# Sums through x's page by ScalarE, S1 and S2 ahead of two transposes, weights in one piece, one subtraction on VectorE

## The chip, the cores and the metric

One Trainium2 chip, one of its cores. The metric is the time of one execution of the whole program in device microseconds (us); 791.16 us is the median of three runs of the kernel before (791.1 to 791.66). A core has five engines that each work through a queue of their own: TensorE (PE; its weight loads are shown apart as PEld), VectorE (DVE), ScalarE (ACT), GpSimd (POOL) and SyncE (SP, which here only starts DMAs). They wait for one another by semaphores. SBUF is the on-chip memory, PSUM the memory of TensorE's results, in eight banks of 512 float32 columns on 128 partitions.

## The reference

Attention with a mask by blocks of 64, and then a feed-forward part with a gate across positions. 8 batches, 8 heads, 576 positions, 64 columns per head, 512 columns of the model, 1024 of the feed-forward part.

```python
def _attn_ref(q, k, v):
    scores = scale * np.matmul(q, k.transpose(0, 1, 3, 2))
    mask = block_i >= block_j                      # pos // 64
    scores = np.where(mask, scores, -1000000000.0)
    attn = np.exp(scores - np.max(scores, axis=-1, keepdims=True))
    attn = attn / (np.sum(attn, axis=-1, keepdims=True) + 1e-09)
    return np.matmul(attn, v)

def _moe_ref(x, w_in, g_ln, w_sg, b_sg, w_out):
    h = gelu(x @ w_in)                             # the tanh form
    u, v = h[..., :512], h[..., 512:]
    v_n = (v - mean(v)) / np.sqrt(var(v) + 1e-06) * g_ln
    v_s = np.einsum('ts,bsd->btd', w_sg, v_n) + b_sg[None, :, None]
    return x + (u * v_s) @ w_out
```

## The kernel before

**Slots.** The program has 32 slots, one for each pair of heads of a batch. Slot n turns the exponents of pair n into its attention output and computes the scores of pair n+1; four slots make a batch. After each batch its feed-forward part is laid out in pieces (`hole`), which the next slots spread between their attention steps. So the first four slots hold attention alone, and from the fifth on every slot has products of the feed-forward part between its steps.

**Accuracy.** Scores and feed-forward products are made of three passes of a fast format: high part by high part, high by low and low by high. For q and k the high part `qk_h` is a CAST on DVE of both together (1152 columns), and the low part `qk_l` is the difference, two subtractions of 576 columns on POOL (`split_qk`, lines 127 to 135). It is made in slot n for pair n+2, so the scores of the next slot need it. A pair's q and k come in by two DMAs on SP, issued at the start of slot n for pair n+2.

**A slot's steps on PE.** `turn0`: the first column block of the exponents of both heads is transposed into two banks named pa (a bank for each head, four transposes each). `turn2`: the third and fourth column blocks into pb. S1 and S2 (`step1`, `step2`): scores of the next pair, into banks s. Block 0 (`av0`): value product with the first column block, into ob. `turn1`: the second and last column blocks into pc. `turn_first`: the two 64x64 corners into pd. S3 and S4: the rest of the next pair's scores. `av2`: value products of pb. `turn_sums`: the inverse row sums, spread over columns by POOL in `rx`, are transposed into pd (128 columns) and pe (512). `av1`: value products of pc. `av00`: the corner's product, also into pd. Each transposed bank is copied to SBUF as pt: pa, pb of the first head by ACT and of the second by DVE, both pc by ACT. Scores get their row maximum on DVE (CUSTOM_DVE, six for S1 and S2, six for S3 and S4), then their exponential on ACT (prob).

**Banks.** Five PSUM banks carry the tag s (scores, ob, accumulators of the feed-forward part), three the tag p (pa, pb, pc, pd, pe, in turn). A new tile of a tag waits until the third tile of p before it, or the fifth of s, has been read for the last time.

**End of a slot.** `normalise` (line 492): ACT copies ob and pd's corner product into a page x, and DVE multiplies x by the inverse sums in pe and pd. `split` makes a high part xh of x on DVE (CAST) and low parts on POOL, for the feed-forward part. SP writes x out to spill.

**Weights.** The feed-forward weights come in during the first nine slots (`WS`, line 731, steps per slot: 2, 2, 2, 1, 10, ...). A weight step fetches a piece by DMA four steps ahead, and unpacks it: `w_in` and `w_out` are double precision, so ACT scales the high words (w<-raw), DVE shifts and merges (TENSOR_SCALAR and two SCALAR_TENSOR_TENSOR on 256 columns), ACT casts the high part (wi_h<-w) and POOL subtracts the low part (wi_l). `load_share` hands a slot's steps out at four places in quarters.

**Order.** PE runs in program order, pinned (`kept`). DVE, ACT, POOL and SP are ordered by a scheduler that takes what it expects to be ready first, within data and buffer dependences; `issue_after` keeps a weight step behind the latest maximum and exponential.

Of the kernel before, what the change touches and what calls it, by code (L numbers as in the profile page):

```python
# [9 lines left out]
F32 = mybir.dt.float32  # L10
# [4 lines left out]
ALU = mybir.AluOpType  # L15
# [13 lines left out]
def kernel(  # L29
# [13 lines left out]
    B, H, D, S = qT.shape  # L43
    P = 128
    BLK = 64
# [23 lines left out]
    def page(dtype, n, name):  # L69
        tag, bufs = KINDS.get(name, KINDS["w"])  # L70
        return sp.tile([P, n], dtype, tag=tag, name=name, bufs=bufs)

    def bank(tag, name, bufs):
        return psum.tile([P, 512], F32, tag=tag, name=name, bufs=bufs)

    def sbank(name):
        return bank("s", name, 5)

    def pbank(name):
        return bank("p", name, 3)  # L80
# [3 lines left out]
    def pin(ins, e):  # L84
        return tc.keep_in_program_order(ins) if e in kept else ins
# [4 lines left out]
    def turn(out, in_, identity):  # L90
        return pin(nc.tensor.transpose(out, in_, identity), "P")  # L91
# [11 lines left out]
    V, A, G, SP = Pinned(nc.vector, "V"), Pinned(nc.scalar, "A"), Pinned(nc.gpsimd, "G"), Pinned(nc.sync, "S")  # L103

    def copy(e, dst, src):
        return {"v": V.tensor_copy, "a": A.copy, "g": G.tensor_copy}[e](dst, src)
# [8 lines left out]
    def load_qk(n):  # L115
        b, h = PAIRS[n]
        if n == 0:

            q_f, k_f = page(F32, S, "w"), page(F32, S, "w")
        else:  # L120
            t = sp.tile([P, 2, S], F32, tag="qk_f", name="qk_f", bufs=1)
            q_f, k_f = t[:, 0, :], t[:, 1, :]
        SP.dma_start(q_f, qT[b, h : h + 2].rearrange("a d s -> (a d) s"))
        SP.dma_start(k_f, kT[b, h : h + 2].rearrange("a d s -> (a d) s"))
        qk[n] = (q_f, k_f) if n == 0 else t

    def split_qk(n):
        t = qk[n]
        hi = sp.tile([P, 2, S], F32R, tag="qk_h", name="qk_h", bufs=1)
        lo = sp.tile([P, 2, S], F32R, tag="qk_l", name="qk_l", bufs=1)  # L130
        V.tensor_copy(hi, t)
        for i in (1, 0):
            G.tensor_tensor(lo[:, i, :], t[:, i, :], hi[:, i, :].bitcast(F32), op=ALU.subtract)
        q_h, k_h, q_l, k_l = hi[:, 0, :], hi[:, 1, :], lo[:, 0, :], lo[:, 1, :]
        qk[n] = [(q_h, k_h), (q_h, k_l), (q_l, k_h)]

    def load_v(n):
        b, h = PAIRS[n]
        v_f = v_bufs[n % 2]
        cols = slice(h * D, (h + 2) * D)  # L140
        SP.dma_start(
            v_f[:, : NT - 1, :],
            v[b, : (NT - 1) * P, cols].rearrange("(j p) d -> p j d", p=P),
        )
        SP.dma_start(v_f[:TAIL, NT - 1, :], v[b, S - TAIL :, cols])
        vals[n] = v_f
# [6 lines left out]
    t = sbank("warm")  # L153
# [15 lines left out]
    for s in (0, 1):  # L169
        t = cp.tile([P, NT, 2 * D], F32, name=f"v_f{s}")  # L170
# [5 lines left out]
    for s in range(4):  # L176
        row = []
        for i in range(NT):
            t = cp.tile([P, P * (i + 1) if i else BLK], F32, name=f"prob{s}_{i}")
# [106 lines left out]
    def weight_step():  # L286

        with ExitStack() as stack:
            for ins in newest.values():
                stack.enter_context(tc.issue_after(ins.ins))  # L290
            while weights and next(weights[0][1], None) is None:
                weights.popleft()
# [96 lines left out]
    class Values:  # L389
# [71 lines left out]
        def turn_sums(self):  # L461

            turn(self.t4[:, 128:256], self.rx[:, 0, :], ident)
            t = self.rp = pbank("pe")
            for i in range(1, NT):
                turn(t[:, (i - 1) * P : i * P], self.rx[:, i, :], ident)

        def av(self, dst, j, pts, c0, n, start, stop):
            for a in (0, 1):
                r = slice(a * D, (a + 1) * D)  # L470
                mm(dst[r, :], self.v[:, j, r], pts[a][:, c0 : c0 + n], start=start, stop=stop)
# [19 lines left out]

        def normalise(self):

            x = self.x = page(F32, S, "x")
            copy("a", x[:, BLK:], self.ob)
            copy("a", x[:, :BLK], self.o0)
            V.tensor_tensor(x[:, BLK:], self.rp, x[:, BLK:], op=ALU.mult)
            V.tensor_tensor(x[:, :BLK], self.t4[:, 128:192], x[:, :BLK], op=ALU.mult)
            spill[self.b, self.p] = dp.tile([P, S], F32, tag="spill", name="spill", bufs=12)
            SP.dma_start(spill[self.b, self.p], x)  # L500

# [14 lines left out]
    def run_side(k):  # L516

        while k > 0 and side and side[0][0] != "G":
            k -= 1
            side.popleft()[1]()  # L520

    def run_gelu():

        if side and side[0][0] == "G":
            side.popleft()[1]()
# [196 lines left out]
    def hole(k=1):  # L722

        while k > 0 and work:
            try:
                next(work[0])
                k -= 1
            except StopIteration:
                work.popleft()

    WS = [2, 2, 2, 1, 10, 3, 3, 3, 2]

    def load_share(n, k):

        if n < len(WS):
            for _ in range(WS[n] * (k + 1) // 4 - WS[n] * k // 4):
                weight_step()

    PLAN = ["1111111", "1111111", "1111111", "1111112"]
# [3 lines left out]
    def slot(n, sc):  # L743
        va = Values(n, sc)
        nx = Scores(n + 1) if n + 1 < N else None
        g = [int(x) for x in (FIRST if n // 4 == 1 else PLAN)[n % 4]]
        if n + 2 < N:
            load_qk(n + 2)
        if n + 1 < N:
            load_v(n + 1)  # L750
        va.inverse()
        va.turn0(0)
        va.turn0(1)
        hole(g[0])
        load_share(n, 0)
        run_side(2)

        va.turn2()
        va.turn2_rest()
        if nx:  # L760
            nx.step1()
            nx.step2()
        va.av0()
        if nx:
            nx.exponents(1, 4)
        va.turn1()
        hole(g[1])
        load_share(n, 1)
        run_side(2)
        hole(g[2])  # L770
        run_side(2)
        va.turn1_rest()
        va.turn_first()
        if nx:
            nx.step3()
            nx.step4()
        va.av2()
        va.turn_sums()
        if nx:
            nx.exponents(3, 0, 2)  # L780
        hole(g[3])
        load_share(n, 2)
        run_side(2)
        va.av1()
        va.av00()
        hole(g[4])
        va.normalise()

        wait = n // (H // 2) > 0 and n % (H // 2) < 2
        pending.append(va.split)  # L790
        if not wait:
            while pending:
                pending.popleft()()
        run_side(2)
        if n + 2 < N:
            split_qk(n + 2)
        load_share(n, 3)
        hole(g[5])
        run_gelu()
        run_side(3)  # L800
        hole(g[6])
        run_side(3)
        if n % (H // 2) == 1:
            while pending:
                pending.popleft()()
        return nx
# [13 lines left out]
    sc.step4()  # L820
    sc.exponents(2)
    split_qk(1)
    for _ in range(2):
        weight_step()
    kept.difference_update("VA")
    for n in range(N):
        sc = slot(n, sc)
        if n % (H // 2) == H // 2 - 1:

            def begin(b=PAIRS[n][0]):  # L830
                v_, u_, s_, o_ = feed_forward(b)

                work.extend([v_, u_, *last_o, s_])
                last_o[:] = [o_]

            begin()
# [45 lines left out]
```

## Time and profile before

| | |
|---|---|
| median of three runs | 791.16 us (791.1 to 791.66) |
| the profiled execution | 792.08 us, of which the span from first to last instruction 790.2 us |
| mean granted clock of PE | 0.978 of full speed |
| PE busy | 761.1 us, 96% |
| DVE busy | 499.7 us, 63% |
| ACT busy | 450.0 us, 57% |
| POOL busy | 267.9 us, 34% |

The durations in this document are from the one profiled execution. A row of the timeline is: start, duration, engine, line, operation, output<-inputs, shape, count, and in brackets the idle time before it and what ended it. All instructions that the kernel issues through its helpers carry the helper's line (L88 products, L91 transposes, L101 the other engines), so they are told apart by tile names. A row of the windows is: start and end, then the length, and busy time with the number of instructions for PE, PEld, DVE, ACT and POOL, the granted clock, the DMA share and GB/s. A row of the waits is: who waited, for whom, total us, how often, and the longest. A row of the groups is: line, engine, operation, tiles, shapes, count, busy us, mean ns, and the idle time before.

### The profile page before, as it was taken

The page shows a single profiled execution, that of the slowest core. Times are in us where ns is not written, and L with a number is a line of the kernel's source. Part 1 is how long each engine was busy: PE and PEld are TensorE (multiplying, and loading weights), DVE is VectorE, ACT ScalarE, POOL GpSimd, SP SyncE. Part 2 cuts the span into 40 slices and gives each one's busy share as a digit, 9 for nine tenths or more (in the row PEclk, how much of TensorE's full clock was granted, in tenths as well). Part 3 has the DMA queues.
Part 4 walks back from the last instruction along what each step waited for, and adds up shares of the span by engine and source line. Part 5 has one row for each costly group of instructions (what it writes and reads, how often), then busy time and mean ns, then how long its engine had stood idle before and what let it go on. Part 6 is the DMA issues. An engine that isn't in the chain of part 4 may idle for free. (4 is left out here: it accounts for less than half of the span.)

```text
span 790.2 us, 15821 instructions
## 1 busy us (share of the span) xinstructions
PE 761.1 (96%) x5926; PEld 639.9 (81%) x5926; DVE 499.7 (63%) x1457; ACT 450.0 (57%) x1172; POOL 267.9 (34%) x331
## 2 busy tenths in 40 slices
PE   7777998999999999999999999999999999999998
PEld 5554786877888888887888888888888978888998
DVE  5897578885757466563866648565676647633532
ACT  4775689567844478435974368544793358721600
POOL 4354255552424113351133414231233510322121
PEclk9897799999999999999999999999999999999999
DMA  7143224212241024311042122410233101320042
GB/s 239 61 126 118 89 91 141 88 61 75 78 149 60 2 76 122 106 61 52 25 136 90 61 76 62 145 50 32 77 106 121 61 19 59 105 76 31 1 121 75
DMA packets 46911, 65.66 MB, mean 83 GB/s; under 512 B 4082, under 2 KB 22514, under 8 KB 46836
## 3 DMA queue, kind: packets, MB, share of 16 engines
q1 hardware_dynamic: 46836, 64.67, 25.6%
q8 instruction: 46, 0.75, 0.4%
q14 instruction: 29, 0.24, 0.1%
HBM read 45.78 MB, written 18.87 MB: 82 GB/s over the span
## 5 line engine op out<-in xcount | busy, mean ns | idle before, releaser
L101 ACT ACTIVATE prob<-prob,negm 128x448 f32<-128x448 f32 (+4 forms) x320 | 176.4, 554 | 40.6 <-DVE negm L101 37.1
L101 POOL TENSOR_TENSOR qk_l<-qk_f,qk_h 128x576 fp32r<-128x576 f32 x62 | 90.9, 1486 | 229.7 <-PE pe L91 92.2
L101 DVE CUSTOM_DVE_ANT_0 prob<-s,mask 128x288 f32<-128x288 f32 (+2 forms) x320 | 117.1, 421 | 56.3 <-PE s L88 56.1
L88 PE MATMUL ob<-pt,v_f 128*64 128x512 f32 (+4 forms) x640 | 107.1, 448 | 0.0
L88 PE MATMUL s<-qk_h 64*128 64x288 f32 (+1 forms) x372 | 88.4, 341 | 3.9 <-ACT u L101 3.7
L101 POOL TENSOR_TENSOR gl<-u,gh 128x288 fp32r<-128x288 f32 x64 | 51.9, 812 | 113.4 <-DVE gh L101 80.2
L88 PE MATMUL s<-qk_l,qk_h 64*128 64x288 f32 (+1 forms) x372 | 83.0, 303 | 0.0
L88 PE MATMUL accu<-xh,wi_h 128*128 128x288 f32 x256 | 78.1, 305 | 0.0
L88 PE MATMUL accs<-ws_h,vh 128*128 128x288 f32 x256 | 78.1, 305 | 0.0
L88 PE MATMUL s<-qk_h,qk_l 64*128 64x288 f32 (+1 forms) x372 | 78.0, 300 | 0.0
L88 PE MATMUL acco<-gh,wo_h 128*128 128x288 f32 x256 | 77.6, 303 | 0.0
L88 PE MATMUL accu<-xl,wi_h 128*128 128x288 f32 x256 | 75.7, 296 | 0.0
L88 PE MATMUL accu<-xh,wi_l 128*128 128x288 f32 x256 | 75.5, 295 | 0.0
L88 PE MATMUL accs<-ws_l,vh 128*128 128x288 f32 x256 | 75.5, 295 | 0.0
L88 PE MATMUL accs<-ws_h,vl 128*128 128x288 f32 x256 | 75.5, 295 | 0.0
L88 PE MATMUL acco<-gh,wo_l 128*128 128x288 f32 x256 | 75.4, 294 | 0.0
L88 PE MATMUL acco<-gl,wo_h 128*128 128x288 f32 x256 | 75.3, 294 | 0.0
L88 PEld LDWEIGHTS ob<-pt,v_f 128*64 128x64 f32 x640 | 37.8, 137 | 41.2 <-issue 32.2
L88 PE MATMUL accv<-wi_h,xh 128*128 128x512 f32 x160 | 66.0, 412 | 3.3 <-POOL xh L101 3.3
L88 PEld LDWEIGHTS s<-qk_h 64*128 64x128 f32 x372 | 63.7, 188 | 5.9 <-ACT u L101 4.9
L88 PEld LDWEIGHTS s<-qk_h,qk_l 64*128 64x128 f32 x372 | 63.8, 187 | 0.0
L88 PE MATMUL accv<-wi_l,xh 128*128 128x512 f32 x160 | 63.8, 399 | 0.0
(104 smaller groups left out, 1924.2 us busy)
## 6 DMA issues: line engine op xcount, KB each, us to landing
spill<-x SPq DMA_DIRECT2D x32, 288.0 KB, 3.7
xr<-spill SPq DMA_DIRECT2D x32, 288.0 KB, 3.2
out_T<-xr SPq DMA_DIRECT2D x32, 288.0 KB, 3.0
qk_f<-in_qT SPq DMA_DIRECT2D x31, 288.0 KB, 3.4
qk_f<-in_kT SPq DMA_DIRECT2D x31, 288.0 KB, 3.8
v_f<-in_v SPq DMA_DIRECT2D x32, 256.0 KB, 3.1
raw<-in_w_in SPq DMA_DIRECT2D x16, 256.0 KB, 4.7
raw<-in_w_out SPq DMA_DIRECT2D x8, 256.0 KB, 5.2
```

The source lines that it names most:

```text
L88: return pin(nc.tensor.matmul(*a, **k), "P")
L101: return lambda *a, **k: pin(f(*a, **k), self.letter)
```

## The change

Four edits, in three groups. In `split_qk` the two subtractions on POOL become one on DVE over both halves. In `turn_sums` the transposed sums are copied by ACT from pe and pd into the page x at once, and `normalise` then multiplies x by ob and by the corner product on DVE, with nothing left for ACT; before, ACT copied ob and the corner, and DVE multiplied by pe and pd. In the first four slots `turn2` stands behind S1, S2 and block 0 rather than ahead of them, and a slot's weight steps are all handed out at the second place rather than in quarters.

```diff
@@ split_qk
-        for i in (1, 0):
-            G.tensor_tensor(lo[:, i, :], t[:, i, :], hi[:, i, :].bitcast(F32), op=ALU.subtract)
+        V.tensor_tensor(lo, t, hi.bitcast(F32), op=ALU.subtract)
@@ turn_sums
-            t = self.rp = pbank("pe")
+            t = pbank("pe")
             for i in range(1, NT):
                 turn(t[:, (i - 1) * P : i * P], self.rx[:, i, :], ident)
+
+            x = self.x = page(F32, S, "x")
+            copy("a", x[:, BLK:], t)
+            copy("a", x[:, :BLK], self.t4[:, 128:192])
@@ normalise
-            x = self.x = page(F32, S, "x")
-            copy("a", x[:, BLK:], self.ob)
-            copy("a", x[:, :BLK], self.o0)
-            V.tensor_tensor(x[:, BLK:], self.rp, x[:, BLK:], op=ALU.mult)
-            V.tensor_tensor(x[:, :BLK], self.t4[:, 128:192], x[:, :BLK], op=ALU.mult)
+            x = self.x
+            V.tensor_tensor(x[:, BLK:], self.ob, x[:, BLK:], op=ALU.mult)
+            V.tensor_tensor(x[:, :BLK], self.o0, x[:, :BLK], op=ALU.mult)
@@ load_share
-            for _ in range(WS[n] * (k + 1) // 4 - WS[n] * k // 4):
+            share = WS[n] * (k + 1) // 4 - WS[n] * k // 4
+            if n < H // 2:
+
+                share = WS[n] if k == 1 else 0
+            for _ in range(share):
                 weight_step()
@@ slot
-        va.turn2()
-        va.turn2_rest()
+        early = n < H // 2
+        if not early:
+            va.turn2()
+            va.turn2_rest()
         if nx:
             nx.step1()
             nx.step2()
         va.av0()
+        if early:
+            va.turn2()
+            va.turn2_rest()
```

In the three places shown next, numbers behind a name (prob_3_132, v_f_105) tell one buffer from another, and x2 means two such instructions in a row.

On PE, at the start of the second slot, before, from the last pa to pc:

```order
L91 MATMUL pa<-ident,prob_1_137 128x128
L91 MATMUL pb<-ident,prob_4_134 128x128
L91 MATMUL pb<-ident,prob_3_132 128x128
...
L91 MATMUL pb<-ident,prob_3_141 128x64
L88 MATMUL s<-qk_h 128x288 x2
...
L88 MATMUL s<-qk_h,qk_l 128x288 x2
L88 MATMUL ob<-pt,v_f_105 64x512 x2
L91 MATMUL pc<-ident,prob_4_134 128x128
```

The same place now:

```order
L91 MATMUL pa<-ident,prob_1_137 128x128
L88 MATMUL s<-qk_h 128x288 x2
...
L88 MATMUL s<-qk_h,qk_l 128x288 x2
L88 MATMUL ob<-pt,v_f_105 64x512 x2
L91 MATMUL pb<-ident,prob_4_134 128x128
L91 MATMUL pb<-ident,prob_3_132 128x128
...
L91 MATMUL pb<-ident,prob_3_141 128x64
L91 MATMUL pc<-ident,prob_4_134 128x128
```

The ten transposes into pb now stand between block 0's product and pc; nothing else on PE has moved.

On ACT, from the end of the first slot into the second, before (x<-ob and x<-pd are the copies of `normalise`):

```order
L101 ACTIVATE w<-raw 128x256
L101 COPY x<-ob 128x512
L101 COPY x<-pd 128x64
L101 COPY pt<-pa 128x512
L101 CAST wi_h<-w 128x256
L101 COPY pt<-pb 128x512
L101 ACTIVATE prob_1_110,sums<-prob_1_110,negm 128x192
L101 ACTIVATE prob_1_119,sums<-prob_1_119,negm 128x192
L101 ACTIVATE prob_4_116,sums<-prob_4_116,negm 128x576
L101 ACTIVATE prob_4_125,sums<-prob_4_125,negm 128x576
L101 ACTIVATE w<-raw 128x256
L101 COPY pt<-pc 128x512 x2
```

The same place now:

```order
L101 COPY x<-pe 128x512
L101 COPY pt<-pa 128x512
L101 ACTIVATE prob_1_110,sums<-prob_1_110,negm 128x192
L101 ACTIVATE prob_1_119,sums<-prob_1_119,negm 128x192
L101 ACTIVATE prob_4_116,sums<-prob_4_116,negm 128x576
L101 ACTIVATE prob_4_125,sums<-prob_4_125,negm 128x576
L101 ACTIVATE w<-raw 128x256 x2
L101 COPY pt<-pb 128x512
L101 COPY pt<-pc 128x512
L101 CAST wi_h<-w 128x256
L101 COPY pt<-pc 128x512
```

The copy of pb, which stood ahead of the four exponentials, now stands behind them and behind two weight steps' first operation; the weight operations around the slot's start are gone.

On DVE, at the same place in the second slot, before:

```order
L101 CAST qk_h<-qk_f 128x1152
L101 TENSOR_SCALAR w<-raw 128x256
L101 SCALAR_TENSOR_TENSOR w<-raw,w 128x256
L101 TENSOR_TENSOR ri<-sums,tiny 128x10
L101 RECIPROCAL ri<-ri 128x10
L101 SCALAR_TENSOR_TENSOR w<-w 128x256
L101 TENSOR_TENSOR x<-pe,x 128x512
L101 TENSOR_TENSOR x<-pd,x 128x64
L101 CAST xh<-x 128x576
L101 COPY pt<-pa 128x512
L101 COPY pt<-pb 128x512
```

The same place now, up to the first maximum of S1:

```order
L101 CAST qk_h<-qk_f 128x1152
L101 TENSOR_TENSOR qk_l<-qk_f,qk_h 128x1152
L101 TENSOR_TENSOR x<-pd,x 128x64
L101 TENSOR_TENSOR ri<-sums,tiny 128x10
L101 TENSOR_TENSOR x<-ob,x 128x512
L101 RECIPROCAL ri<-ri 128x10
L101 COPY pt<-pa 128x512
L101 CAST xh<-x 128x576
L101 ISA prob_4_116,negm<-s,mask 128x288
```

The low part's subtraction is new behind the CAST, the three weight operations and the copy of pb have left this stretch, and the multiplies read ob and pd's corner. The copy of pb stands here behind the six maxima and three weight operations, at this place:

```order
L101 ISA prob_4_125,negm<-s,mask,negm 128x288
L101 ISA negm 128x1
L101 TENSOR_SCALAR w<-raw 128x256 x2
L101 SCALAR_TENSOR_TENSOR w<-raw,w 128x256
L101 COPY pt<-pb 128x512
L101 SCALAR_TENSOR_TENSOR w<-raw,w 128x256
L101 SCALAR_TENSOR_TENSOR w<-w 128x256 x2
L101 ISA prob_3_114,negm<-s,mask 128x448
```

Two weight steps now follow one another there, where before one stood alone.

## Prediction

> **What bounds the kernel now.** I read the clock row of the page first, then a long window from the middle, then the list of what TensorE waited for.
>
> ```profile
> PEclk9897799999999999999999999999999999999999
> ...
> 300.00:400.00 100.00, 99.56 (x800) 84.94 (x799) 63.55 (x183) 60.19 (x154) 35.92 (x41) 1.00 0.26 82
> ...
> PE pa L91 <- ACT pt L101: 6.1, 4, 1.9
> PE pb L91 <- DVE x L101: 3.7, 3, 1.4
> ...
> PE accv L88 <- POOL xh L101: 3.3, 1, 3.3
> ```
>
> Each digit of the first row is 20 us: the granted clock is below full only in the first seven slices. In the window from 300 to 400 TensorE (PE, first pair of numbers) is busy 99.56 of 100 us at clock 1.00, with DVE at 64 and ACT at 60. So from about 140 us on, nothing but PE's own work sets the end, and the change adds or removes no product. What can move is the start: the four slots without feed-forward products, and the fifth. Time won before PE is full is won once and kept.
>
> The slots are measured from one first product of S3 to the next. A name is tile<-operands, then shape, count, and in brackets the idle time before it and what ended it.
>
> ```profile
> 14.44 1.71 PE L91 MATMUL pb<-ident,prob 128*128 128x128 f32 x7
> 15.87 0.42 PE L88 MATMUL s<-qk_h 64*128 64x288 f32 x1
> ...
> 17.46 1.08 PE L88 MATMUL ob<-pt,v_f 128*64 128x512 f32 x4
> 18.47 1.08 PE L91 MATMUL pc<-ident,prob 128*128 128x128 f32 x7
> ...
> 20.07 0.47 PE L88 MATMUL s<-qk_h 64*128 64x448 f32 x1 [0.19 <-DVE negm L101]
> ...
> 37.24 0.45 PE L88 MATMUL s<-qk_h 64*128 64x448 f32 x1
> ...
> 38.84 1.08 PE L88 MATMUL ob<-pt,v_f 128*64 128x320 f32 x8
> ...
> 41.68 0.66 PE L91 MATMUL pa<-ident,prob 128*128 128x128 f32 x4
> 43.64 0.66 PE L91 MATMUL pa<-ident,prob 128*128 128x128 f32 x4 [1.30 <-ACT pt L101]
> 45.61 1.08 PE L91 MATMUL pb<-ident,prob 128*128 128x128 f32 x7 [1.31 <-DVE x L101]
> ...
> 51.48 0.44 PE L88 MATMUL s<-qk_h 64*128 64x448 f32 x1
> ...
> 65.82 0.44 PE L88 MATMUL s<-qk_h 64*128 64x448 f32 x1
> ...
> 78.83 0.80 PE L88 MATMUL accv<-wi_h,xh 128*128 128x512 f32 x1 [3.26 <-POOL xh L101]
> ```
>
> S3 stands at 20.07, 37.24, 51.48 and 65.82: periods of 17.2, 14.2 and 14.3. At full clock the pieces are S1+S2 1.6 (15.87 to 17.46), block 0's products 1.0 (to 18.47), S3+S4 1.6, from there to the next pa 2.8 (38.84 to 41.68), and some 3 for the transposes: about 10. The rest is the pair of waits at each slot's start (1.30 and 1.31 here) and the half clock after them. In the third group the two waits have these causes:
>
> ```profile
> 38.37 0.62 DVE L101 CUSTOM_DVE_ANT_0 prob<-s,mask 128x448 f32<-128x448 f32 x1 [0.62 <-PE s L88]
> ...
> 40.57 0.75 DVE L101 CAST qk_h<-qk_f 128x1152 fp32r<-128x1152 f32 x1
> ...
> 41.56 1.58 DVE L101 SCALAR_TENSOR_TENSOR w<-raw,w 128x256 uint32<-128x256 uint32 x1
> 43.07 1.36 DVE L101 TENSOR_TENSOR ri<-sums,tiny 128x10 f32<-128x10 f32 x1
> ...
> 41.45 2.95 POOL L101 TENSOR_TENSOR qk_l<-qk_f,qk_h 128x576 fp32r<-128x576 f32 x2 [1.57 <-PE pe L91]
> ...
> 39.03 0.67 ACT L101 ACTIVATE prob<-prob,negm 128x448 f32<-128x448 f32 x1
> ...
> 42.44 0.56 ACT L101 COPY x<-ob 128x512 f32<-128x512 f32 x1
> 43.01 0.58 ACT L101 COPY pt<-pa 128x512 f32<-128x512 f32 x1
> ```
>
> While POOL subtracts (41.45 to 44.40), two DVE operations that read SBUF take 1.58 and 1.36, the second for ten columns. They stand in front of the multiply by pe, which frees pe's PSUM bank for pb. The second pa waits for ACT's copy of the first, since pd and pe hold the other two banks.
>
> **The change, part by part.** (1) *Low parts on DVE.* POOL's 2.95 goes, and with it the two held operations, about 2.2 per slot on DVE. DVE gets one subtraction of 1152 columns, which no row shows. Below it stands the CAST of that width (0.75), above it POOL's 2.95. I work it out from one DVE operation in two widths:
>
> ```profile
> L101 DVE CUSTOM_DVE_ANT_0 prob<-s,mask 128x448 f32<-128x448 f32 x64 | 39.5, 617 | 47.2 <-PE s L88 47.0
> ...
> L101 DVE COPY pt<-pb 128x512 f32<-128x512 f32 x32 | 21.9, 685 | 7.2 <-PE pb L91 6.6
> ...
> L101 DVE CUSTOM_DVE_ANT_0 prob<-s,mask 64x64 f32<-64x64 f32 x64 | 13.5, 211 | 0.0
> ```
>
> (617-211)/384 is 1.06 ns a column and 0.14 fixed, so 1.36, nearer the CAST than POOL. At 0.75 each of three slots would gain 0.6 more; at 2.95 each would lose 1.6.
>
> (2) *Sums through x's page.* The same two ACT copies, of pd and pe now, before the exponents end; pe's bank comes free on ACT, before DVE's multiply. New waits: the last product into pd follows ACT's copy of pd, and the next block-0 product needs DVE's multiply of ob. Walked from S3 at 0 (DVE's first maximum at 1.13 and CAST at 3.33, ACT's first exponent at 1.79, all from the rows above): ACT copies pd at about 4.5 and pe at 5.5, DVE ends the subtraction at 5.3, the pd multiply at 5.5, ob's at 6.2. PE would reach the last pd product at 4.3 and waits 0.3; the second pa waits 0.3 for pe's copy; S1 starts at 6.0 with q and k split. Two waits of 1.3 become two of 0.3. Behind the subtraction on DVE stand the copy of the second pa and the cast of x, so the maxima start at about 7.3.
>
> (3) *S1 and S2 before pb.* Maxima start earlier, but pb is now copied late: in ACT's order its copy stands behind four exponents and two weight multiplies, in DVE's behind six maxima, two shifts and one merge. pc's second half takes the bank that DVE's copy frees.
>
> ```profile
> 33.47 0.46 DVE L101 CUSTOM_DVE_ANT_0 prob<-s,mask 128x288 f32<-128x288 f32 x1 [0.52 <-PE s L88]
> ...
> 35.66 0.29 DVE L101 TENSOR_SCALAR w<-raw 128x256 uint32<-128x256 uint32 x1
> 35.99 0.43 DVE L101 SCALAR_TENSOR_TENSOR w<-raw,w 128x256 uint32<-128x256 uint32 x1
> ...
> 34.25 0.46 ACT L101 ACTIVATE prob<-prob,negm 128x192 f32<-128x192 f32 x1 [1.26 <-DVE negm L101]
> ...
> 36.88 0.41 ACT L101 ACTIVATE w<-raw 128x256 f32<-128x256 f32 x1
> ```
>
> Six maxima take 2.2 (33.47 to 35.66), two shifts and a merge about 1.0, the copy 0.69: from 7.3 that is 11.2. PE, after S1, S2, block 0 and pb, has only three transposes of pc left and stands from 9.95 to 11.25: a **new wait of 1.3** in mid-slot. ACT's copy (exponents from 0.78 behind the first maximum, 2.63 long, two multiplies 0.7, copy 0.58) is done at 12.0 and just frees pd. S3 comes at 12.35. That is the second slot's successor: 12.35 against 14.24.
>
> (4) *First slot.* Here pc's second half needs ACT's copy of pb. S1 starts at 14.44, where pb stood; PE is through S1, S2, block 0, pb and half of pc at 19.2. DVE copies the second pa at 14.7 and has two weight pieces to unpack, so maxima run from 17.25 to 19.8, exponents to 21.0, two multiplies to 21.7, a CAST that waits for DVE to 22.2, the copy to 22.8. **PE waits 3.7 us**; S3 moves from 20.07 to 23.75.
>
> (5) *Slots after it.* The slot behind that wait runs S3 at half clock until 26.1: 13.1 instead of 17.17. The next 12.35 instead of 14.24. In the fourth slot one weight step is left, with one DVE cast and no ACT work ahead of the copies: 11.75 instead of 14.34. S3 of the fourth slot: 23.75+13.1+12.35+11.75 = 60.95 against 65.82, won 4.9. There the feed-forward block waits for POOL's xh, before 13.0 behind S3; now three shifts, the subtraction, the merges and three weight splits on POOL lead to 12.45, won 0.5. Behind it stands half clock before (the row of 80.70 below); it becomes shorter, and I count 0.3. Hand-overs that the walk leaves out cost 0.1 in each of four slots. Sum: 4.9+0.5+0.3-0.4 = **5.3 us**. From the profiled execution (792.08 with a span of 790.2) that is 786.8; the median of the runs shown lies 0.92 lower, so **785.9**. The later 28 slots I count at 0, within 1 either way: a block of products stands between each new wait and the work that it holds. Input loads on SP still run one slot ahead of their use.
>
> **Rivals.** (a) *The clock.* The granted clock goes in steps of 3.4 us:
>
> ```profile
> 12.40:15.80 3.40, 2.69 (x12) 2.42 (x12) 2.10 (x4) 2.02 (x8) 2.95 (x4) 0.52 0.20 74
> ...
> 22.60:26.00 3.40, 2.30 (x21) 1.33 (x19) 3.37 (x15) 3.40 (x13) 0.83 (x2) 1.00 0.01 2
> 26.00:29.40 3.40, 1.09 (x6) 0.62 (x6) 3.36 (x5) 2.31 (x8) 3.06 (x4) 1.00 0.29 87
> 29.40:32.90 3.50, 2.83 (x20) 2.50 (x22) 2.81 (x6) 0.91 (x2) 2.98 (x4) 0.53 0.75 246
> ...
> 43.10:46.50 3.40, 1.55 (x12) 1.14 (x13) 3.33 (x8) 0.89 (x3) 2.81 (x4) 1.00 0.54 162
> ...
> 80.70:84.10 3.40, 3.40 (x27) 2.79 (x26) 2.28 (x7) 0.74 (x3) 0.00 (x0) 0.50 0.86 328
> ```
>
> A step with PE busy 1.09 or 1.55 is followed by half clock, one with 2.30 is not. The new wait leaves about 2.1 of 3.4, between them. If it costs the next step, S3 and S4 run at half clock and each of three periods grows by 0.85: 2.5 lost, less 1.0 since the fifth slot's half clock lies partly in its wait: 787.4. The Trainium skill's page "TensorE: Matmul & The Clock Gate", Part 4 (PE-mode transpose), says that transposes do not count as PE work for the clock; by that rule the stretch of pb, wait and pc counts as idle and this rival holds, at 787.4. This case speaks both ways: the step at 12.40 holds transposes alone and full clock follows (pb to 15.87, S1 then at 0.42), the step at 29.40, half transposes, is followed by more half clock.
>
> (b) *The lock moves.* POOL's split of x (576 columns, half of the 2.95) now runs beside DVE's maxima and ends about where the shifts start. If it ends later, shift and merge are held as 1.58 and 1.36 show: 1.3 in each of three slots, won 1.4: 789.8. The page "SBUF — State Buffer", section "SBUF: two separate sides", calls it an exclusive lock for whole instructions; the trace agrees.
>
> (c) *Slower: the wait for pb's copy is as long in each slot as in the first.* It decides from 1.3+1.8 = 3.1 us a slot on. At 3.7, and 0.85 for the half clock, three slots lose 9.75 more: 795.6. For it: ACT's in-order queue and weights in mid-slot. Against it: from the second slot on the bank hangs on DVE's copy, which stands ahead of most unpacking.
>
> (d) *More.* If the fifth slot loses one step of half clock less (3.4 us at half speed, 1.7) and the subtraction takes the CAST's 0.75 (three slots by 0.6, 1.8): 3.5 more, 782.4.
>
> **Chances.** Forecast 0.42, clock 0.20, more 0.13, lock 0.13, slower 0.12. A measurement here can tell about 0.2% (1.6 us). Forecast, clock and more count as faster, 0.75; lock as the same, 0.13; slower 0.12. The range 781.5 to 790.5 leaves out the slower case and the far ends, under 2 in 10.
>
> **What would show it.** pa's second wait and S1's start near 0.3 instead of 1.3; no pb wait for DVE; a wait of pc for DVE's or ACT's pt of 3 to 4 us in the first slot and 1 to 1.5 in the next three; S3 of the fourth slot near 61; DVE's qk_l at 1.36; the clock row of the third to fifth slice above 7. I am wrong if pc waits over 3 in later slots, if the subtraction takes near 3, or if PE below 99% appears after 140 us.

## The result and the profile after

The changed kernel takes 784.45 us (median of four runs, 783.3 to 785.17) against 791.41 us of the kernel before measured with it (791.1 to 791.82): a ratio of 0.991, interval 0.9896 to 0.9925. That is 7.0 us won where 5.3 were forecast. The profiled execution took 783.98 us, its span is 782.2. The page of the changed kernel opens with:

```profile
span 782.2 us, 15752 instructions
...
PE 756.5 (97%) x5926; PEld 636.9 (81%) x5926; DVE 497.0 (64%) x1488; ACT 448.1 (57%) x1172; POOL 182.5 (23%) x269
...
PEclk8898999999999999999999999999999999999999
```

POOL is 85 us less busy. DVE now does the subtraction in 42 us and yet is no busier than before (497.0, before 499.7). The clock row is still below full only in the first seven slices.

PE's waits in the first five slots of the changed kernel, by its timeline, with the first product of S3 of each slot between them:

```profile
23.14 1.20 PE L91 MATMUL pc<-ident,prob 128*128 128x128 f32 x4 [2.61 <-ACT pt L101]
...
24.17 0.72 PE L88 MATMUL s<-qk_h 64*128 64x448 f32 x1
...
36.88 0.94 PE L91 MATMUL pc<-ident,prob 128*128 128x128 f32 x7 [0.88 <-DVE pt L101]
...
37.88 0.47 PE L88 MATMUL s<-qk_h 64*128 64x448 f32 x1
...
49.18 0.94 PE L91 MATMUL pc<-ident,prob 128*128 128x128 f32 x7 [1.02 <-DVE pt L101]
...
50.09 0.47 PE L88 MATMUL s<-qk_h 64*128 64x448 f32 x1
...
55.21 0.34 PE L88 MATMUL pd<-pt,v_f 128*64 128x64 f32 x4 [0.77 <-ACT x L101]
...
61.11 0.75 PE L91 MATMUL pc<-ident,prob 128*128 128x128 f32 x4 [0.53 <-DVE pt L101]
...
61.73 0.45 PE L88 MATMUL s<-qk_h 64*128 64x448 f32 x1
...
74.46 0.80 PE L88 MATMUL accv<-wi_h,xh 128*128 128x512 f32 x1 [4.77 <-POOL xh L101]
```

The pair of waits of 1.3 at each slot's start is gone from the second slot on; what remains there is 0.8 or less. In its place stands the wait of pc in mid-slot, 2.61 in the first slot and 0.5 to 1.0 after it. From S3 to S3 a slot takes 13.7, 12.2 and 11.6 us instead of 17.8, 14.2 and 14.3.

### The profile page after: what moved, and what is told of

The parts are those of the page before. It is cut to its first block, busy times and chain, and to the rows that moved or that the text cites. A ratio compares the mean times of both kernels' runs of the same rounds, so it can differ in the third digit from the quotient of the medians.

```text
span 782.2 us, 15752 instructions
## 1 busy us (share of the span) xinstructions
PE 756.5 (97%) x5926; PEld 636.9 (81%) x5926; DVE 497.0 (64%) x1488; ACT 448.1 (57%) x1172; POOL 182.5 (23%) x269
## 5 line engine op out<-in xcount | busy, mean ns | idle before, releaser
L88 PE MATMUL s<-qk_h 64*128 64x288 f32 (+1 forms) x372 | 84.2, 338 | 3.7 <-ACT u L101 3.7
L88 PE MATMUL s<-qk_l,qk_h 64*128 64x288 f32 (+1 forms) x372 | 78.6, 299 | 0.0
L88 PE MATMUL s<-qk_h,qk_l 64*128 64x288 f32 (+1 forms) x372 | 73.6, 296 | 0.0
L101 DVE TENSOR_TENSOR xr<-acco,xr 128x288 f32<-128x288 f32 x64 | 29.2, 457 | 60.7 <-PE acco L88 50.5
L101 ACT COPY pt<-pa 128x512 f32<-128x512 f32 x32 | 18.6, 580 | 85.6 <-PE pa L91 85.6
L88 PEld LDWEIGHTS s<-qk_h 64*128 64x128 f32 x372 | 60.1, 184 | 6.3 <-ACT u L101 5.1
L101 DVE TENSOR_TENSOR u<-accs,u 128x288 f32<-128x288 f32 x64 | 29.2, 456 | 56.4 <-PE accs L88 56.2
```

The costliest lines, as they stand in the source:

```text
L88: return pin(nc.tensor.matmul(*a, **k), "P")
L101: return lambda *a, **k: pin(f(*a, **k), self.letter)
```

## The experiments

The four edits are called **low** (low parts on DVE), **sums** (sums copied by ACT from pe and pd), **late pb** (pb behind block 0) and **one piece** (weights at one place) here. The table has the median with its range, the ratio to the kernel before of the same session with its interval, the start of S3 in the first slot, and the next three periods from S3 to S3 in the profiled execution. Starts differ by up to 1.1 us between executions already at the first transposes (11.05 to 12.16), so the periods compare better than the starts. For the first slot the table has S3's first product; the 20.07 that the prediction starts from is the second head's, 0.65 behind it.

| kernel | edits in it | us (range) | ratio (interval) | first S3 | periods |
|---|---|---|---|---|---|
| before | none | 791.41 (791.1–791.82) | 1 | 19.42 | 17.8, 14.2, 14.3 |
| changed | all four | 784.45 (783.3–785.17) | 0.991 (0.9896–0.9925) | 24.17 | 13.7, 12.2, 11.6 |
| e1 | all but low | 784.63 (784.45–787.13) | 0.9921 (0.9908–0.9933) | 25.42 | 13.3, 12.5, 11.9 |
| e2 | all but sums | 785.33 (784.43–789.03) | 0.9925 (0.9909–0.994) | 24.39 | 14.5, 12.4, 11.8 |
| e3 | all but late pb | 777.98 (777.94–778.59) | 0.9828 (0.9816–0.9841) | 22.08 | 10.7, 11.8, 11.8 |
| e4 | all but one piece | 783.3 (783.27–783.35) | 0.9894 (0.9881–0.9907) | 24.70 | 12.8, 12.0, 12.0 |
| e5 | low alone | 784.87 (782.73–785.98) | 0.9921 (0.9902–0.9939) | 20.07 | 13.7, 13.6, 13.6 |
| e6 | all, first slot without late pb and one piece | 780.06 (779.62–780.49) | 0.9861 (0.9845–0.9877) | 20.42 | 14.0, 12.6, 11.6 |
| e7 | all, first slot without late pb | 781.75 (780.03–783.0) | 0.9884 (0.9866–0.9901) | 20.36 | 14.7, 12.2, 11.6 |
| e8 | late pb alone | 792.07 (790.63–794.58) | 1.0003 (0.9994–1.0013) | 24.20 | 15.0, 14.2, 13.9 |
| e9 | sums alone | 781.75 (779.97–782.16) | 0.9873 (0.9857–0.9889) | 19.51 | 13.2, 12.9, 12.9 |
| e10 | low and sums | 778.54 (778.1–781.24) | 0.9837 (0.9822–0.9853) | 19.64 | 12.9, 11.8, 12.1 |
| e11 | e3, first feed-forward piece one step later | 781.5 (781.03–782.03) | 0.9865 (0.9849–0.9882) | 20.64 | 12.9, 11.8, 11.8 |
| e12 | e11 with 15 more transposes in the first slot | 780.75 (780.32–781.77) | 0.986 (0.9845–0.9874) | 22.17 | 11.0, 11.8, 11.8 |

### One edit undone at a time (e1 to e4)

The theories were A, that relieving DVE of POOL's hold is most of the gain, and B, that the order of pb, S1 and the sums is.

**e1, low parts on POOL again.**

```diff
-        V.tensor_tensor(lo, t, hi.bitcast(F32), op=ALU.subtract)
+        for i in (1, 0):
+            G.tensor_tensor(lo[:, i, :], t[:, i, :], hi[:, i, :].bitcast(F32), op=ALU.subtract)
```

> The changed kernel with the low parts of q and k again as two subtractions on POOL; all else as changed. Theory A (the relief of DVE is most of the gain: the ten-column addition falls from 0.75 to 0.17 us when POOL's 2.9 us are gone): about 2 us come back in each of the first slots and the two half-clock stretches with them, 789 to 790 us, DVE busy back above 510 minus the 42 of the subtraction, and the wait of pb for DVE's pt in the sixth slot near 2 again. Theory B (the order of pb, S1 and the sums is most of it): only 1 to 2.5 us come back, 785.5 to 787.

784.63: nothing comes back, against both theories. With the other three edits in place POOL's two subtractions cost PE a short wait in S1 and no more, once each in the second to fourth slot, first here:

```profile
33.27 0.40 PE L88 MATMUL s<-qk_h,qk_l 64*128 64x288 f32 x2 [0.59 <-POOL sums L101]
```

(The product reads qk_l; the profile names the POOL instruction that ended next to it.)

**e2, sums as before.** `turn_sums` and `normalise` are taken back to the old text shown in the diff of the change.

> The changed kernel with turn_sums and normalise as before (ACT copies ob and the corner, DVE multiplies by pe and pd). Theory A: the multiply by pe is no longer held, so 1 to 2 us come back, 785.5 to 786.5. Theory B: the wait of S1 or pb for the bank of pe returns, about 1.0 us in each of three slots plus some half clock, 787.5 to 789.

785.33, the same as the changed kernel within the two ranges, and just below what theory A gave. Two edits that each can be taken away without loss: either they do nothing, or something else caps the gain.

**e3, pb ahead of S1 and S2 again.**

```diff
-        early = n < H // 2
+        early = False
```

> The changed kernel with pb ahead of S1 and S2 in all slots. The waits of pc in mid-slot (2.6, 0.9, 1.0 and 0.5 us) go; a wait of pb for the multiply or for ACT's copy at the slot's start takes their place. Theory A: that wait is under 0.7 us in each slot since DVE is free early, 783 to 785, S3 of the fourth slot at 60 to 62. Theory B: the wait is 1.0 to 1.3 and half clock follows it, 786.5 to 788.5, S3 of the fourth slot at 63 to 64.5.

777.98, 6.5 us less than the changed kernel and below what either theory gave. Late pb is the cap, and it costs nearly as much as the whole change wins.

**e4, weights in quarters again.** The three lines of `load_share` that gather the shares are taken out.

> The changed kernel with the weight steps of the first four slots in quarters again. Theory A (weights matter little once POOL does not hold DVE): within 1 us of the changed kernel, 783.5 to 785.5. Theory B (weight work at the slot's start sits before the copies that free the banks): 1.5 to 3 us come back, 786 to 787.5, with waits over 0.7 us at the slots' starts.

783.3: 1.2 us less than the changed kernel, at the edge of its range (783.3 to 785.17). One piece gains nothing here.

### What low is worth, and where late pb loses (e5 to e7)

**e5, low alone.** The edit of `split_qk` made in the kernel before.

> The kernel before with one edit: the low parts of q and k in one subtraction on DVE. Theory A (relief of DVE is most of the gain): 4 us or more of the 7 come, 786 to 787.5; the second wait at each slot's start (pb for DVE's x, 1.3) falls below 0.5. Theory B (order): 1 to 2.5 us, 789 to 790.5, and the two waits at the slot's start stay near 1.

784.87: by itself this edit gives 6.5 us, almost all that the change gives and more than either theory. PE no longer waits for the multiply of x in these slots, but pa's wait for ACT's copy stays, as in the third and fourth slot here, where half clock still comes with it (from 40.8 and from 54.5, one step of 3.4 us each):

```profile
41.14 1.11 PE L91 MATMUL pa<-ident,prob 128*128 128x128 f32 x4 [1.49 <-ACT pt L101]
...
54.69 1.12 PE L91 MATMUL pa<-ident,prob 128*128 128x128 f32 x4 [1.48 <-ACT pt L101]
```

**e6, the first slot as before in pb and weights.**

```diff
-        early = n < H // 2
+        early = 0 < n < H // 2
-            if n < H // 2:
+            if 0 < n < H // 2:
```

> The changed kernel with the first slot as before in two points: pb ahead of S1 and S2, weights in quarters. The wait of pc for ACT's copy of pb (2.6 us) and the half clock after it go. If the loss of the first slot is won time once it is avoided: S3 of the first slot near 20 instead of 24.2, 3 to 4 us less in the fourth slot, 780.5 to 782.5. If later waits (accv for POOL's xh, 4.8) take it up: 783.5 to 785.

780.06: 4.4 us less than the changed kernel, and just below the first expectation. So late pb and one piece together lose 4.4 in the first slot, where S3 starts at 20.42 instead of 24.17 although this execution began 0.96 later (first transposes at 12.01 and 11.05).

**e7, only the first line of e6.**

> As the last one, but with the first slot's weights still in one piece at the second place: only pb goes back ahead of S1 and S2 in the first slot. If the order of pb alone made the wait of 2.6 us: the same time as the last kernel, within 1 us. If the two weight pieces on DVE and ACT make it: pc or av2 waits over 1 us in the first slot again and the time is 783 to 785.

781.75, between the two expectations, with ranges that overlap e6's (780.03 to 783.0 and 779.62 to 780.49). The position of pb in the first slot is worth 2.7 by the medians; that the weights in one piece cost something there is likely (PE waits 1.37 for ACT's copy of pd's corners there, 1.04 in e6) but not settled by these runs. Left in the second to fourth slot alone, late pb still costs 3.8: e3 differs from e7 in nothing else (777.98 and 781.75).

### The other edits alone (e8 to e10)

The theories are now C, that each edit has a worth of its own, negative for late pb, and D, that edits pay or cost only beside the others.

**e8, late pb alone.** The edit of `slot` made in the kernel before.

> The kernel before with one edit: pb behind S1, S2 and block 0 in the first four slots. Theory C (pb late costs in itself: a wait of pc of 2 to 4 us in the first slot, and 0.5 to 1 in the next three): the later S1 start is won and the first slot lost, 789 to 793 us, S3 of the first slot near 24. Theory D (pb late gains 3 us or more when low parts and sums are as before, and only loses beside them): 785 to 788.5.

792.07 with a ratio of 1.0003: no gain, as theory C gave. In its first slot:

```profile
23.17 1.20 PE L91 MATMUL pc<-ident,prob 128*128 128x128 f32 x4 [2.32 <-ACT pt L101]
...
24.20 0.72 PE L88 MATMUL s<-qk_h 64*128 64x448 f32 x1
```

S3 comes at 24.20, just as in the changed kernel (24.17), and 4.8 us later than before (19.42). The next three periods win 3.3 of that back (15.0 instead of 17.8 in the second), and the fifth slot the rest (24.8 us from S3 to S3 instead of 27.4).

**e9, sums alone.** The edits of `turn_sums` and `normalise` made in the kernel before, low parts on POOL.

> The kernel before with one edit: the sums copied by ACT from pe and pd, multiplied by DVE with ob. Theory C (the sums free pe's bank without DVE and are worth 3 us or more by themselves): 784 to 788. Theory D (DVE, held by POOL's two subtractions, is the bound of the first slots, and the sums pay only with it relieved): 789 to 791.5.

781.75: 9.8 us from this edit alone, more than from the whole change and more than theory C gave. The pair of waits at the third slot's start, 1.30 and 1.31 before, becomes one for ACT's copy of pd and a short one. A wait for ACT's copy of pd's corners, ahead of the sums' transposes, is new in this slot:

```profile
36.62 0.30 PE L91 MATMUL pd<-ident,rx 128*128 128x128 f32 x1 [1.04 <-ACT pt L101]
...
39.45 0.34 PE L88 MATMUL pd<-pt,v_f 128*64 128x64 f32 x4 [1.08 <-ACT x L101]
...
40.70 0.66 PE L91 MATMUL pa<-ident,prob 128*128 128x128 f32 x4 [0.33 <-DVE x L101]
```

The granted clock stays full from the first slot's S3 to the fourth's, and the periods fall to 12.9. Theory D falls for this edit: it pays while POOL still subtracts.

**e10, low and sums, nothing else.**

> The kernel before with two edits: low parts on DVE and the sums; pb ahead of S1 and weights in quarters as before. Theory C (the two carry all of the gain, the other two edits cost): 776 to 779 us, as fast as the run with pb first or faster. Theory D (weights in one piece are needed for the 778): 780 to 784, with waits at the slots' starts over 0.7.

778.54, not to be told from e3's 777.98. Low (6.5) and sums (9.8) together win about 13, less than their sum, since both end the same pair of waits. These two carry the gain. Late pb takes 6.5 of it beside one piece (changed kernel and e3) and 4.8 beside quarters (e4 and e10); one piece takes nothing that the runs can tell.

### What bounds the faster version (e11, e12)

The windows from S3 to S3 of the third slot show what is left: length, then PE, PEld, DVE, ACT and POOL. The kernel before:

```profile
37.24:51.48 14.24, 11.62 (x99) 7.90 (x100) 12.61 (x38) 9.49 (x30) 6.88 (x8) 0.88 0.45 139
```

The changed kernel:

```profile
37.88:50.09 12.21, 10.86 (x97) 7.18 (x97) 11.03 (x39) 9.81 (x32) 4.50 (x7) 1.00 0.48 150
```

e3:

```profile
32.77:44.58 11.81, 10.41 (x99) 6.92 (x100) 11.14 (x40) 9.74 (x32) 4.70 (x7) 1.00 0.41 127
```

In e3 DVE is busy 11.14 of 11.81 us, 94%, and PE 10.41: in these slots DVE, and not PE, has the least room left, and that it is the bound is read from this share. Before, DVE was busy 12.61 without the subtraction, since some of it was spent held by POOL (the rows of 1.58 and 1.36 in the prediction).

**e11, the first feed-forward piece one step later.** In e3 PE waits for POOL's xh in the fifth slot, as the changed kernel does at 74.46:

```profile
69.11 0.80 PE L88 MATMUL accv<-wi_h,xh 128*128 128x512 f32 x1 [4.42 <-POOL xh L101]
```

```diff
-    FIRST = ["1111111", "1111101", "0011011", "1011010"]
+    FIRST = ["0111111", "1111101", "0011011", "1011010"]
```

> The run with pb first (all edits but that one), and the first feed-forward piece of the fifth slot left to the second place (the fifth slot starts with pb, S1, S2 and block 0). If PE's wait of 4.4 us for POOL's xh and the half clock behind it are lost time: 3 to 5 us less than the run with pb first, 773 to 775, with no wait for xh over 1 us. If DVE's and ACT's queues of the fifth slot are late anyhow, another wait takes its place: 777 to 778.5.

781.5, about 3 us slower than e3 (3.5 by the medians, 2.9 by the ratios). The wait for xh is gone, but the moved piece makes the chain of the gate late two slots on. The waits of e11 that are new against e3:

```profile
PE accs L88 <- ACT vh L101: 7.4, 2, 7.2
PE pd L91 <- ACT pt L101: 6.6, 4, 4.5
```

PE stands 7.2 us for the scaled v (vh) and 4.5 for the copy of pd's corners (ACT ends it at 121.51, PE goes on at 121.65), which on ACT stands behind both copies of pc and parts of the GELU. Between the parts of the GELU and the exponentials ACT loads its function table each time, four times in 10 us, the first and the last:

```profile
115.34 1.28 ACT L101 ACT_TABLE_LOAD   x1
...
124.09 1.28 ACT L101 ACT_TABLE_LOAD   x1
```

So this way of ending the wait for xh moves the loss two slots on and makes it larger. Whether another order of the pieces could win the 4.4 is open.

**e12, fifteen transposes in the first slot's gaps.**

```diff
                 self.turn(a, t[:, (i - 1) * P : i * P], i, 0)
+                if self.n == 0 and a == 0 and i > 2:
+                    for _ in range(6 if i == 4 else 9):
+                        turn(t[:, :P], ident, ident)
```

> As the last one, with 15 transposes of the identity between the first slot's first transposes, in the two gaps of 1.1 and 1.5 us after which the clock fell to half (their values are overwritten by the real ones). If transposes count as work for the clock: no half clock from 12 to 22 us, S3 of the first slot near 19.7 instead of 22.1, and 1 to 2.5 us less than the last one, unless DVE is the bound of the second slot, which gives 0 to 1. If they do not count: half clock stays, the same time as the last one within 0.7 us.

780.75 against 781.5, ranges that overlap (780.32 to 781.77, 781.03 to 782.03). The clock of the steps around the gaps, in e11:

```profile
10.60:14.00 3.40, 0.81 (x4) 0.28 (x2) 3.37 (x14) 3.40 (x15) 0.00 (x0) 1.00 0.66 222
14.00:17.40 3.40, 3.38 (x22) 2.92 (x24) 2.90 (x8) 1.73 (x5) 0.99 (x2) 0.58 0.51 161
```

and in e12:

```profile
10.20:13.60 3.40, 2.51 (x19) 1.82 (x17) 3.37 (x14) 3.40 (x15) 0.00 (x0) 1.00 0.79 263
13.60:17.00 3.40, 1.67 (x12) 1.26 (x12) 3.29 (x8) 2.12 (x7) 1.74 (x3) 1.00 0.52 161
17.00:20.40 3.40, 3.40 (x26) 2.77 (x26) 3.02 (x12) 1.44 (x4) 0.73 (x1) 0.53 0.80 243
```

With PE busy 0.81 half clock comes in the next step; with 2.51, nearly all of it transposes, it does not. But in the next step the second pb waits 1.64 for ACT's copy, PE is busy 1.67, and half clock comes one step later. S3 of the first slot comes later than in e11 (22.17, 20.64), and the next period makes it up (11.0, 12.9): in the second slot PE is not the bound. What the fill is worth these two runs don't tell.

## Why the prediction came out as it did

**The size of DVE's subtraction** was right: 1.36 forecast from one operation in two widths, 1.353 measured. The held operations went as forecast: POOL's subtractions gone, DVE has about 45 us less of its old work (499.7 + 41.9 - 497.0), or 1.4 a slot over 31 slots; the 2.2 of the prediction is a slot with a weight merge beside the subtraction. The addition of ten columns takes 643 to 752 ns on average in all four kernels that still subtract on POOL (before, e1, e8, e9) and 160 to 177 in the ten that do not. Before,

```profile
L101 DVE TENSOR_TENSOR ri<-sums,tiny 128x10 f32<-128x10 f32 x32 | 24.0, 751 | 22.8 <-ACT prob L101 21.5 <-POOL qk_l L101 1.3
```

and after, with the new subtraction:

```profile
L101 DVE TENSOR_TENSOR qk_l<-qk_f,qk_h 128x1152 fp32r<-128x1152 f32 x31 | 41.9, 1353 | 0.7
...
L101 DVE TENSOR_TENSOR ri<-sums,tiny 128x10 f32<-128x10 f32 x32 | 5.4, 167 | 1.7 <-ACT prob L101 1.7
```

**The first slot** was nearly right as a time: S3 forecast at 23.75, its first product measured at 24.17. The wait is 2.61 instead of 3.7, because half clock kept PE until 20.5 where 19.2 was assumed; ACT's copy of pb ends at 23.1, forecast 22.8. As a loss it was forecast too small. The prediction moves S3 from 20.07, which is the second head's product; from the first one, at 19.42, the slot loses 4.75 and not 3.7, and the second slot's period before is 17.8 and not 17.2. In the sum up to the fourth slot the two cancel. **The three periods** were forecast at 13.1, 12.35 and 11.75 and are 13.71, 12.21 and 11.64. The first is longer than forecast since half clock follows the first slot's wait for two steps, to 29.2, where 26.1 was assumed. The granted clock (the number ahead of the last two) in the first slot and behind it:

```profile
12.40:15.80 3.40, 2.89 (x18) 2.56 (x20) 2.58 (x7) 1.82 (x6) 0.20 (x2) 0.50 0.48 150
15.80:19.20 3.40, 3.40 (x18) 1.52 (x17) 3.37 (x11) 1.60 (x5) 1.56 (x2) 0.53 0.85 292
...
22.60:26.00 3.40, 2.86 (x23) 2.50 (x24) 0.50 (x1) 2.02 (x6) 1.45 (x2) 0.50 0.02 5
26.00:29.40 3.40, 3.40 (x19) 1.93 (x18) 3.27 (x14) 2.62 (x10) 0.00 (x0) 0.53 0.00 0
```

The waits of pc, 1.3 forecast, are 0.88, 1.02 and 0.53. Up to S3 of the fourth slot 4.9 were forecast won, and 4.1 are.

**Two terms of the sum were too small.** The fifth slot was to bring 0.5 + 0.3 and brings 1.6: S3 behind it stands at 87.48, 5.7 ahead of before (93.19). The product that waits for xh starts 4.4 ahead of before (74.46 and 78.83), 0.3 more than S3 in front of it, where 0.5 was forecast. The other 1.3 is half clock. It sets in ahead of that product in both kernels, but behind the product's start it lasts 6.0 us, where it lasted 8.8 before. After:

```profile
73.86:77.28 3.42, 2.82 (x13) 2.19 (x15) 0.68 (x1) 0.58 (x1) 1.92 (x3) 0.50 0.86 314
77.28:80.69 3.41, 3.41 (x25) 2.43 (x23) 2.55 (x12) 1.57 (x5) 0.00 (x0) 0.54 0.04 12
80.69:84.10 3.41, 3.41 (x19) 2.64 (x18) 2.43 (x8) 3.03 (x10) 0.47 (x1) 1.00 0.15 21
```

Before, behind the step at half clock that the prediction shows (80.70 to 84.10):

```profile
84.10:87.51 3.41, 3.41 (x12) 1.80 (x12) 2.47 (x12) 3.14 (x11) 0.00 (x0) 0.50 0.00 0
87.51:90.92 3.41, 3.41 (x17) 2.77 (x16) 2.44 (x6) 1.95 (x5) 1.93 (x3) 0.98 0.32 89
```

That the edits shorten it is not shown. The fifth slot takes 22.4 to 25.6 us from S3 to S3 in the single profiled executions of e1 to e10, and 24.8 in e8, which has neither low nor sums.

And the later slots were counted at 0, where the seventh brings 2.1 (S3 5.9 ahead in the slot before, 8.0 behind it). Before, pb waited there for DVE's copy and the clock halved:

```profile
130.86 0.75 PE L91 MATMUL pb<-ident,prob 128*128 128x128 f32 x4 [2.15 <-DVE pt L101]
```

```profile
128.47:131.88 3.41, 1.26 (x16) 0.85 (x16) 3.41 (x6) 3.07 (x5) 2.69 (x3) 1.00 1.02 338
131.88:135.30 3.42, 3.42 (x21) 1.79 (x18) 3.42 (x12) 3.40 (x7) 1.75 (x2) 0.52 0.67 223
```

After, the wait is half as long and the clock stays:

```profile
123.91 0.75 PE L91 MATMUL pb<-ident,prob 128*128 128x128 f32 x4 [1.11 <-DVE pt L101]
```

```profile
121.45:124.86 3.41, 2.30 (x24) 1.89 (x24) 3.41 (x6) 3.00 (x5) 2.62 (x3) 1.00 0.96 291
124.86:128.27 3.41, 2.93 (x28) 1.88 (x26) 3.27 (x10) 3.39 (x7) 1.91 (x2) 1.00 0.70 266
```

The runs show what it takes: with low and sums together the wait is 1.1 (e3, e4, e6, e7, e10), with neither 2.2 (e8, and before), with the sums and no low 2.2 (e1, e9), with low and no sums 3.2 (e2, e5). (The expectation of e1 calls this slot the sixth.) The sum left this wait out because it lies outside the four slots that the edits name. Two of the four edits act in all 32 slots. About half of the 2.1 is this wait, and the other half the step of half clock: e8 waits 2.17 there and yet keeps full clock, and its slot takes 20.5 us, before 21.6, the changed kernel's 19.5. That the change ended the half clock there is therefore not shown.

These terms (4.1, 1.6 and 2.1) make 7.8 of the 8.0 us between the two profiled spans. The medians lie 7.0 apart: the profiled execution of before took longer than its median (792.08 and 791.41), that of the changed kernel less (783.98 and 784.45). That the forecast of 785.9 comes within 1.5 us of the median is in part luck: the first four slots won less than forecast (4.1, where 4.9 less 0.4 for hand-overs were counted), and the later ones 2.9 more, much of it half clock that the sum did not see.

**Rivals.** The clock (a) did not follow the new wait in the later slots; it followed only the first slot's. In the third slot the step at 46.56 with PE busy 2.39 is followed by full clock:

```profile
46.56:49.97 3.41, 2.39 (x20) 1.76 (x19) 3.41 (x13) 3.30 (x11) 1.22 (x2) 1.00 0.98 347
49.97:53.39 3.42, 3.42 (x38) 2.44 (x36) 2.31 (x12) 3.36 (x11) 1.46 (x2) 1.00 0.35 135
```

The Trainium skill's page "TensorE: Matmul & The Clock Gate", Part 4 (PE-mode transpose), by which transposes do not count as busy in the same way, is not borne out here for keeping full clock: in e12 the step from 10.20, filled with transposes, kept it, and the measurement decides. For getting it back this case speaks both ways, as the prediction says: the first slot's step of transposes at half clock is followed by full clock before (from 15.9) and by two more steps at half clock in e3 (to 22.5). The lock (b) did not move. In the third slot of the changed kernel POOL splits x while DVE takes its maxima:

```profile
45.85 1.41 POOL L101 TENSOR_TENSOR xl<-x,xh 128x576 fp32r<-128x576 f32 x1
```

```profile
46.07 0.45 DVE L101 CUSTOM_DVE_ANT_0 prob<-s,mask 128x288 f32<-128x288 f32 x1
...
48.11 0.41 DVE L101 SCALAR_TENSOR_TENSOR w<-raw,w 128x256 uint32<-128x256 uint32 x1
```

The maxima keep their 0.45 (0.46 at 33.47 before) and the merge behind takes 0.41, not 1.58. The Trainium skill's page "SBUF — State Buffer", section "SBUF: two separate sides", says that against such work of POOL an operation of DVE is held when it has two SBUF inputs. The rows agree: the maxima have one, the mask, and read the scores from PSUM. The slower case (c) did not come: pc waits 1.02 or less after the first slot. Of (d) the shorter half clock of the fifth slot came in the profiled execution (1.3 won by it, 1.7 on top of 0.3 forecast), and the subtraction took 1.35 rather than the CAST's 0.75.

**What the prediction did not ask** is what each part is worth without the others. It costed late pb by its new waits and had their places right, with sizes of 2.61 and 0.5 to 1.0 instead of 3.7 and 1.3. But it compared the slots only with those of before, where pb, and S1 behind it, still waited for DVE. Once sums and low have ended those waits, moving S1 ahead of pb wins nothing that the runs show, and the loss of 6.5 us remains.

## What to carry to other kernels

When a change has several parts that end the same wait, cost each part also on top of the others: the second and third may win nothing and keep their price, and undoing them one by one shows it (here the best version is the change without late pb, 777.98 us, a ratio of 0.9828). What POOL's work costs DVE is read from DVE's smallest operations, such as an addition of ten columns: here it took four times as long in the kernels where POOL subtracts beside it. And look for waits of the same engine outside the stretch that the edit names, when the edit acts there too.

## What the runs showed of the hardware that was not expected

Half clock can be the smaller loss. e3 and e11 have the same work in the first four slots, in the same order on ACT and DVE. e3 runs the first slot at half clock from 12.3 to 22.5, e11 for one step only (14.6 to 18.0); from the first transposes (11.10 and 12.16) to S3 of the fourth slot (56.35 and 57.05) they take 45.25 and 44.89. Two more steps of 3.4 us at half clock, 3.4 us of PE's work, cost 0.4 there, since the second slot makes the rest up (10.7 and 12.9): there PE is not the bound. Splitting the GELU between exponentials costs ACT 1.28 us for each table load; in e11 one of them (at 118.39) stands between the two copies of pc, ahead of the copy that PE waits for. The start of the first transposes differs by up to 1.1 us between executions of kernels whose code up to there is the same, and with it where PE's gaps fall in the clock's steps of 3.4 us; differences of one such step (1.7 us) between two single executions say nothing of the edit.
